# Row-tiled projections placed between score and value units of an attention + gated-MLP kernel, with a rearranged first head and a four-slot tail

## The chip, the cores and the metric

The kernel runs on one core of one Trainium2 chip. The metric is the device time of one execution in microseconds (us), from the first instruction to the last; a kernel's time is the median of its runs. The engines are PE (TensorE matmuls), PEld (weight loads, which overlap PE), DVE (VectorE), ACT (ScalarE), POOL (GpSimd) and SP (SyncE, which starts DMAs).

## The reference

```python
xn  = layernorm(x)                                   # x: 1 x 2048 x 640, bf16
q   = xn @ wq                                        # 32 heads of 192
p   = softmax(q @ k^T * 192**-0.5)                   # k, v caches: 32 heads x 2048 x 192
s   = concat_heads(p @ v) @ wo
h   = silu(xn @ w1) * (xn @ w3)                      # 640 -> 1536
out = x + s * silu(h @ w2)
```

## The kernel before

The kernel walks over a stream of units `(h, qb, p)`: head, block of 512 queries, pair of 128-key tiles. A block is eight pairs, and there are 32 x 4 = 128 blocks. Per pair, PE computes scores into one slot of a PSUM ring (two slots of two banks, pool `ps_st`), ACT takes the exponential, and two pairs later PE multiplies by the values into `obank`, a PSUM tile of four banks. Scores and values use only 64 rows of the array per matmul, so both run in *row tiles*: matmuls on rows 0 to 63 and on rows 64 to 127 go side by side.

```python
    ps_st = main.enter_context(tc.tile_pool(name="ps_st", bufs=2, space=bass.MemoryType.PSUM))
    ps_o  = main.enter_context(tc.tile_pool(name="ps_o", bufs=1, space=bass.MemoryType.PSUM))

    def project(h, qb, half):                       # full array: 5 matmuls over 128 rows
        ...
        ps = ps_st.tile([P, 1024], F32, tag="st2", name="ps")
        for c in range(DC):
            w = L["wqB"][:, c, :] if half else L["wq"][:, c, 0:P]
            nc.tensor.matmul(ps[:, 0:512], lhsT=w, rhs=xnT[:, c, qs], start=(c == 0), stop=(c == DC - 1))
        if half:
            nc.scalar.copy(out=qAB[:, 1, qs], in_=ps[:, 0:512])
        else:
            nc.vector.tensor_copy(out=qAB[:, 0, qs], in_=ps[:, 0:512])
        ...

    def values(n):
        h, qb, p = stream[n]
        if p == 0:
            obanks[0] = ps_o.tile([P, 2048], F32, tag="ob", name="obank")
        obank = obanks[0]
        ...                                         # 16 matmuls, r = 0 into banks 0-1, r = 1 into banks 2-3
        if p < NPAIR - 1:
            return
        ov = obank[:].rearrange("p (r j w) -> p r j w", r=2, j=4)
        osum = osp.tile([P, 4, DH + 1], F32, tag="osum", name="osum")
        nc.scalar.copy(out=osum[:], in_=ov[:, 0, :, 0:DH + 1])
        nc.vector.tensor_tensor(out=osum[:], in0=ov[:, 1, :, 0:DH + 1], in1=osum[:], op=ALU.add)

    for n, (h, qb, p) in enumerate(stream):
        scores(n + 2)
        values(n)
        ...                                         # head 0: LayerNorm and projection of its next block
        if p < NPAIR - 1:
            continue
        if h + 1 < H:
            project(h + 1, qb, 1)                   # both halves at the end of the block
            project(h + 1, qb, 0)
        finish_values(h, qb)
        if h < 2 * NPIG:
            swiglu(h, qb)                           # even heads: tanh on ACT, product on DVE
        loads_after(h, qb)
```

`obank` has one buffer. The first value unit of a block may therefore start only when both halves of the last block's `obank` have been read.

## Time and profile before

| | before |
|---|---|
| time, median (range of 4 runs) | 2004.1 us (2002.2 to 2005.1) |
| PE busy, granted clock | 98%, 0.994 |
| period of a block, heads 1 to 30 | 12.884 us |
| head 0 (from the start to the score unit of head 1's third pair, the first after all work of head 0) | 100.62 us |
| tail (from the first `ps_gu` matmul at 1692.78 us to the end) | 307.8 us |

The period is the distance of two equal PE rows of neighbouring blocks. From the page of the kernel before, the busy times and the chain of work that ended last:

```profile
PE 1966.2 (98%) x26025; PEld 1306.8 (65%) x26025; DVE 529.0 (26%) x862; ACT 1280.0 (64%) x1403; POOL 329.5 (16%) x561
...
PE 97%; DVE 2%; ACT 1%; issue 0%; DMA 0%; POOL 0%; DVEq 0%; ACTq 0%
```

The next fence is the timeline of PE before, at the end of a block (start in us, length in us, engine, line, operation, output and inputs, shapes, count):

```profile
1024.61 0.38 PE L343 MATMUL st_17867<-qAB,KA 64*128 64x512 bf16 x1
...
1025.26 0.83 PE L373 MATMUL obank<-vt_112,pT_17824 64*128 64x193 bf16 x16
1026.02 1.25 PE L297 MATMUL ps<-xnT,wqB 128*128 128x512 bf16 x5
1027.11 1.24 PE L297 MATMUL ps<-xnT,wq 128*128 128x512 bf16 x5
1028.28 0.39 PE L343 MATMUL st_17925<-qAB,KA 64*128 64x512 bf16 x1
...
1028.94 0.83 PE L373 MATMUL obank<-vt_113,pT_17849 64*128 64x193 bf16 x16
```

Read starts, not lengths, because matmuls are pipelined. A score unit takes 0.65 us, a value unit 0.67 us; from the last value unit of one block (1025.26) to the first of the next (1028.94) are 3.68 us. In that time `obank` must be read. Here is the timeline of ACT and DVE for it, in the same kernel:

```profile
1026.44 0.80 ACT L382 COPY osum<-obank 128x772 f32<-128x772 f32 x1
1027.27 0.96 DVE L383 TENSOR_TENSOR osum<-obank,osum 128x772 f32<-128x772 f32 x1 [9.28 <-ACT osum L382]
```

The bracket gives the idle time before a row and what ended it. The two reads follow each other; the second ends at 1028.23, before PE wants the bank at 1028.94. So in heads 1 to 30 the eviction is free. In head 31, which projects nothing, it isn't. From the list of waits of the kernel before (engine and output, who ended the wait, us in total, times, longest):

```profile
DVE qC L304 <- ACT qAB L299: 11.0, 4, 3.1
ACT ft L526 <- DVE hT L527: 9.9, 16, 0.6
ACT qC L306 <- DVE qAB L301: 6.0, 4, 1.5
PE obank L373 <- DVE osum L383: 4.6, 3, 1.6
```

In head 0, `qC` and `qAB` are both copies of one tile `ps`, and they read the same bank of it. In the tail, a tile `ps_f` has two parts; ACT takes the tanh `ft` of a part and DVE multiplies it into `hT`. The tanh of the second part needs nothing of the first part's product, and yet it waits for it in each of the 16 tiles, 0.62 us.

### The profile page before, as it was taken

The page shows a single profiled execution, that of the slowest core. Times are in us where ns is not written, and L with a number is a line of the kernel's source. Part 1 is how long each engine was busy: PE and PEld are TensorE (multiplying, and loading weights), DVE is VectorE, ACT ScalarE, POOL GpSimd, SP SyncE. Part 2 cuts the span into 40 slices and gives each one's busy share as a digit, 9 for nine tenths or more (in the row PEclk, how much of TensorE's full clock was granted, in tenths as well). Part 3 has the DMA queues.
Part 4 walks back from the last instruction along what each step waited for, and adds up shares of the span by engine and source line. Part 5 has one row for each costly group of instructions (what it writes and reads, how often), then busy time and mean ns, then how long its engine had stood idle before and what let it go on. Part 6 is the DMA issues. An engine that isn't in the chain of part 4 may idle for free.

```text
span 2000.6 us, 57142 instructions
## 1 busy us (share of the span) xinstructions
PE 1966.2 (98%) x26025; PEld 1306.8 (65%) x26025; DVE 529.0 (26%) x862; ACT 1280.0 (64%) x1403; POOL 329.5 (16%) x561
## 2 busy tenths in 40 slices
PE   7999999999999999999999999999999998999998
PEld 4566666666666666666666666666666666567776
DVE  5322222222222222222222222222222222521111
ACT  4677777777777777777777777777777776210000
POOL 2111111111111111111111111111111110000000
PEclk8999999999999999999999999999999999999999
DMA  7123332334333434363434343433233310908873
GB/s 153 34 61 92 65 99 64 95 65 98 68 99 68 99 68 99 67 162 68 100 68 99 68 99 68 97 66 99 68 91 77 64 53 25 253 20 148 152 147 60
DMA packets 361368, 177.43 MB, mean 89 GB/s; under 512 B 307360, under 2 KB 348064, under 8 KB 361120
## 3 DMA queue, kind: packets, MB, share of 16 engines
q1 hardware_dynamic: 335984, 114.96, 26.7%
q0 software_dynamic: 22832, 56.13, 11.7%
q8 instruction: 205, 3.36, 0.8%
q10 hardware_dynamic: 2304, 2.62, 0.5%
q14 instruction: 43, 0.35, 0.1%
HBM read 54.66 MB, written 27.79 MB: 41 GB/s over the span
## 4 chain that ended last, share of the span: by engine, by line
PE 97%; DVE 2%; ACT 1%; issue 0%; DMA 0%; POOL 0%; DVEq 0%; ACTq 0%
PE obank L373 34%; PE ps L297 14%; PE ps_s L102 10%; PE ps_f L521 3%; PE ps_gu L492 1%; PE ps_gu L495 1%; DVE stats L262 0%; PE pst L279 0%; DMA x_all<-in_A_x_dram 0%; DVE qAB L301 0%; DVE osum L383 0%; ACT osum L382 0%; DVE mv L263 0%; ACT qC L306 0%; DVE qC L307 0%
## 5 line engine op out<-in xcount | busy, mean ns | idle before, releaser
L383 DVE TENSOR_TENSOR osum<-obank,osum 128x772 f32<-128x772 f32 x128 | 123.2, 962 | 1178.6 <-ACT osum L382 1178.6
L309 POOL DMA_DIRECT2D qC<-qAB x248 | 132.2, 533 | 1288.4 <-ACT qAB L299 1207.8
L102 PE MATMUL ps_s<-wo_sb,oT 128*128 128x256 bf16 (+1 forms) x1536 | 208.8, 299 | 2.2 <-issue 2.2
L102 PEld LDWEIGHTS <-oT 128*128 128x128 bf16 x1536 | 150.2, 98 | 60.5 <-issue 2.2
L343 PEld LDWEIGHTS <-KC 64*128 64x128 bf16 x1024 | 96.5, 94 | 123.5 <-ACT KC L231 2.0
L297 PE MATMUL ps<-xnT,wqB 128*128 128x512 bf16 x640 | 161.4, 383 | 1.0 <-DVE xnT L282 1.0
L297 PE MATMUL ps<-xnT,wq 128*128 128x512 bf16 x640 | 159.4, 380 | 0.0
L343 PEld LDWEIGHTS <-KA 64*128 64x128 bf16 x1024 | 96.2, 94 | 56.2 <-issue 55.8
L390 DVE TENSOR_TENSOR ostage<-osum,rl_all 128x768 bf16<-128x768 f32 x128 | 122.6, 958 | 4.4
L297 PEld LDWEIGHTS <-wq 128*128 128x128 bf16 x640 | 62.8, 98 | 76.1 <-issue 1.0
L382 ACT COPY osum<-obank 128x772 f32<-128x772 f32 x128 | 102.0, 797 | 0.9 <-PE obank L373 0.9
L344 PEld LDWEIGHTS <-KA 64*128 64x128 bf16 x1024 | 96.1, 94 | 3.6 <-issue 3.5
L344 PEld LDWEIGHTS <-KB 64*128 64x128 bf16 x1024 | 96.6, 94 | 0.4 <-issue 0.4
L343 PEld LDWEIGHTS <-KB 64*128 64x128 bf16 x1024 | 96.6, 94 | 0.3 <-issue 0.3
L344 PEld LDWEIGHTS <-KC 64*128 64x128 bf16 x1024 | 96.5, 94 | 0.0
L297 PEld LDWEIGHTS <-wqB 128*128 128x128 bf16 x640 | 52.3, 98 | 67.2 <-issue 22.2
L301 DVE CAST qAB<-ps 128x512 bf16<-128x512 f32 x128 | 88.6, 692 | 19.3 <-PE ps L297 19.2
L299 ACT CAST qAB<-ps 128x512 bf16<-128x512 f32 x128 | 75.0, 586 | 14.0 <-PE ps L297 5.4
L311 POOL DMA_DIRECT2D qC<-qAB x124 | 65.0, 524 | 0.3 <-issue 0.3
L107 DVE SCALAR_TENSOR_TENSOR tmp<-ps_s,hT 128x384 f32<-128x384 f32 (+1 forms) x32 | 15.6, 488 | 179.6 <-PE ps_s L102 179.6
L521 PE MATMUL ps_f<-w_all,hT 128*128 128x384 bf16 (+1 forms) x384 | 52.3, 299 | 0.0
L98 POOL DMA_DIRECT2D xt<-in_A_x_dram x16 | 8.6, 540 | 256.1 <-DVE res L110 256.1
(9272 smaller groups left out, 5448.1 us busy)
## 6 DMA issues: line engine op xcount, KB each, us to landing
o_scr<-ostage SPq DMA_DIRECT2D x16, 1536.0 KB, 9.3
qC<-qAB POOLq DMA_DIRECT2D x372, 64.0 KB, 1.9
vt_112<-in_A_v_cache_dram SPq DMA_DIRECT2D x16, 768.0 KB, 6.6
vt_113<-in_A_v_cache_dram SPq DMA_DIRECT2D x16, 768.0 KB, 6.4
wq<-in_A_wq_dram POOLq DMA_DIRECT2D x32, 240.0 KB, 3.6
wo_sb<-in_A_wo_dram POOLq DMA_DIRECT2D x1, 7680.0 KB, 39.2
KC<-KA POOLq DMA_DIRECT2D x31, 128.0 KB, 5.8
KC<-KB POOLq DMA_DIRECT2D x31, 128.0 KB, 6.0
```

The source lines that it names most:

```text
L102: nc.tensor.matmul(ps[:, b * 512:b * 512 + c1 - c0], lhsT=oT[:, k, :], rhs=wo_sb[:, k, c0:c1], start=(k == 0), stop=(k == OC - 1))
L297: nc.tensor.matmul(ps[:, 0:512], lhsT=w, rhs=xnT[:, c, qs], start=(c == 0), stop=(c == DC - 1))
L299: nc.scalar.copy(out=qAB[:, 1, qs], in_=ps[:, 0:512])
L301: nc.vector.tensor_copy(out=qAB[:, 0, qs], in_=ps[:, 0:512])
L309: nc.gpsimd.dma_start(out=qC[0:64, half, qs], in_=qAB[64:P, half, qs])
L343: nc.tensor.matmul(st2[:, 0:512], lhsT=k0, rhs=q0, start=r == 0, stop=r == 2)
L344: nc.tensor.matmul(st2[:, 512:1024], lhsT=k1, rhs=q1, start=r == 0, stop=r == 2)
L373: nc.tensor.matmul(obank[:, o0:o0 + DH + 1], lhsT=pT2[r * 64:(r + 1) * 64, t * 512 + j * P:t * 512 + (j + 1) * P], rhs=vt[r * 64:(r + 1) * ...
L382: nc.scalar.copy(out=osum[:], in_=ov[:, 0, :, 0:DH + 1])
L383: nc.vector.tensor_tensor(out=osum[:], in0=ov[:, 1, :, 0:DH + 1], in1=osum[:], op=ALU.add)
L390: nc.vector.tensor_tensor(out=ostage[:, qb * 4:qb * 4 + 4, hg * DH:(hg + 1) * DH], in0=osum[:, :, 0:DH], in1=rl.unsqueeze(2).to_broadcast( ...
L521: nc.tensor.matmul(ps[:, b * 512:b * 512 + c1 - c0], lhsT=hT[:, fc, i * P:(i + 1) * P], rhs=w2_sb[:, fc, c0:c1], start=(fc == 0), stop=(fc ...
```

## The change

The intent: take the changes between row tiles and the full array out of every block by projecting in row tiles, and hide the accumulator's eviction under one half of a projection; give head 0 its LayerNorm statistics a block ahead and a warmed-up PE; use four PSUM slots in the tail.

```diff
 def project(h, qb, half):
         ps = ps_st.tile([P, 1024], F32, tag="st2", name="ps")
+        if h == 0: ...                              # as before
+        else:
+            for c in range(DC):
+                for r in range(2):
+                    rows = slice(r * 64, (r + 1) * 64)
+                    nc.tensor.matmul(ps[:, r * 512:(r + 1) * 512], lhsT=w[rows, c, 0:P], rhs=xnT[rows, c, qs],
+                                     start=(c == 0), stop=(c == DC - 1))
+            part = hbp.tile([P, 512], F32, tag="part", name="part")
+            nc.scalar.copy(out=part[:], in_=ps[:, 0:512])
+            nc.vector.tensor_tensor(out=dst, in0=ps[:, 512:1024], in1=part[:], op=ALU.add)
 ...
         nc.scalar.copy(out=osum[:], in_=ov[:, 0, :, 0:DH + 1])
-        nc.vector.tensor_tensor(out=osum[:], in0=ov[:, 1, :, 0:DH + 1], in1=osum[:], op=ALU.add)
+        nc.vector.tensor_copy(out=opart[:], in_=ov[:, 1, :, 0:DH + 1])
+        nc.vector.tensor_tensor(out=osum[:], in0=osum[:], in1=opart[:], op=ALU.add)
 ...
     for n, (h, qb, p) in enumerate(stream):
         scores(n + 2)
+        if h + 1 < H and p == (5 if h == 0 else 0):
+            project(h + 1, qb, 1)
+        if h + 1 < H and p == (NPAIR - 1 if h == 0 else NPAIR // 2):
+            project(h + 1, qb, 0)
         values(n)
+        if p == 0 and n > 0:
+            finish_block(n - 1)
+        if p == 2 and h < 2 * NPIG:
+            swiglu(h, qb)
         if h == 0 and qb + 1 < NQB:
-            ...
+            if p == 1 or p == 2:
+                ln_norm(qb + 1, p - 1)
+            if p == 3:
+                project(0, qb + 1, 1); project(0, qb + 1, 0)
+            if qb + 2 < NQB and 3 <= p < 7:
+                ln_stats(qb + 2, p - 3)
 # cut: longer PE warm-up, KC copies ahead of the first projection, head 0's qC by DMA from block 1 on;
 # tail: ps_gu, ps_f and ps_s alternate between ps_st and a second pool on obank's banks,
 #       the count matmul moves from after ps_f to its fifth tile, the last output tile is cut 512 + 128
```

More of the change, by code (lines that the diff above doesn't have):

```diff
@@ L90, in _exact_attention, with _output_stage @@
                 nc.sync.dma_start(out=o_scr[qs, bass.ds(h * DH, DH)], in_=ob[:])
-def _output_stage(nc, i, oT, g, wo_sb, x2, out2, sb, ps_pool):
+def _output_stage(nc, i, oT, g, wo_sb, x2, out2, sb, ps_pools, last=False):
     D = out2.shape[1]
     OC = wo_sb.shape[1]
+    cuts = [(0, D - P), (D - P, D)] if last and D - P <= 512 else _column_pieces(D)
     xt = sb.tile([P, D], BF16, tag="xt", name="xt")
     nc.gpsimd.dma_start(out=xt[:], in_=x2[i * P:(i + 1) * P, :])
-    ps = ps_pool.tile([P, 1024], F32, tag="st2", name="ps_s")
-    for b, (c0, c1) in enumerate(_column_pieces(D)):
-        for k in range(OC):
-            nc.tensor.matmul(ps[:, b * 512:b * 512 + c1 - c0], lhsT=oT[:, k, :], rhs=wo_sb[:, k, c0:c1],
-                             start=(k == 0), stop=(k == OC - 1))
     tmp = sb.tile([P, D], F32, tag="tmp", name="tmp")
     res = sb.tile([P, D], BF16, tag="res", name="res")
-    for b, (c0, c1) in enumerate(_column_pieces(D)):
+    for b, (c0, c1) in enumerate(cuts):
+        w = c1 - c0
+        ps = ps_pools[b % len(ps_pools)].tile([P, 1024], F32, tag="st2", name="ps_s")
+        for k in range(OC):
+            nc.tensor.matmul(ps[:, 0:w], lhsT=oT[:, k, :], rhs=wo_sb[:, k, c0:c1], start=(k == 0), stop=(k == OC - 1))
         nc.vector.scalar_tensor_tensor(out=tmp[:, c0:c1].rearrange("p (a w) -> p a w", w=P),
-                                       in0=ps[:, b * 512:b * 512 + c1 - c0].rearrange("p (a w) -> p a w", w=P),
+                                       in0=ps[:, 0:w].rearrange("p (a w) -> p a w", w=P),
                                        scalar=0.5, in1=g[:, c0 // P:c1 // P, :], op0=ALU.mult, op1=ALU.mult)
         nc.vector.tensor_tensor(out=res[:, c0:c1], in0=tmp[:, c0:c1], in1=xt[:, c0:c1], op=ALU.add)
-    nc.scalar.dma_start(out=out2[i * P:(i + 1) * P, :], in_=res[:])
+        if last:
+            nc.scalar.dma_start(out=out2[i * P:(i + 1) * P, c0:c1], in_=res[:, c0:c1])
+    if not last:
+        nc.scalar.dma_start(out=out2[i * P:(i + 1) * P, :], in_=res[:])
 def _column_pieces(n):
@@ L188, in _kernel_impl @@
     hbp = att.enter_context(tc.tile_pool(name="hbp", bufs=2))
-    osp = att.enter_context(tc.tile_pool(name="osp", bufs=2))
+    osp = att.enter_context(tc.tile_pool(name="osp", bufs=1))
     lnp = att.enter_context(tc.tile_pool(name="lnp", bufs=2))
     ps_st = main.enter_context(tc.tile_pool(name="ps_st", bufs=2, space=bass.MemoryType.PSUM))
-    ps_o = main.enter_context(tc.tile_pool(name="ps_o", bufs=1, space=bass.MemoryType.PSUM))
+    ps_o = att.enter_context(tc.tile_pool(name="ps_o", bufs=1, space=bass.MemoryType.PSUM))
     x_all = fw.tile([P, WX], BF16, tag="xw", name="x_all")
@@ L230, in copy_k @@
             nc.scalar.copy(out=KC[64:P, :], in_=KA[0:64, HK:SK])
-            nc.scalar.copy(out=KC[0:64, :], in_=KB[64:P, 0:HK])
+            nc.vector.tensor_copy(out=KC[0:64, :], in_=KB[64:P, 0:HK])
         else:
@@ L252, in _kernel_impl, with ln_stats @@
     lnorm = {}
-    def ln_stats(g):
-        mv = lnp.tile([P, 4, nc.vector.BN_AGGR_DIM], F32, tag="mv", name="mv")
-        ve = lnp.tile([P, 4], F32, tag="ve", name="ve")
-        rstd = lnp.tile([P, 4], F32, tag="rstd", name="rstd")
-        for i in range(4):
-            stats = lnp.tile([P, nsub, nc.vector.BN_STATS_DIM], F32, tag="stats", name="stats")
-            xr = x_sb[:, 4 * g + i, :].rearrange("p (a f) -> p a f", a=nsub)
-            for a in range(nsub):
-                nc.vector.bn_stats(out=stats[:, a, :], in_=xr[:, a, :])
-            nc.vector.bn_aggr(out=mv[:, i, :], in_=stats[:])
-            if i % 2 == 1:
-                two = slice(i - 1, i + 1)
-                nc.vector.tensor_scalar(out=ve[:, two], in0=mv[:, two, 1], scalar1=eps, scalar2=None, op0=ALU.add)
-                nc.gpsimd.tensor_tensor(out=rstd[:, two], in0=ve[:, two], in1=mhalf[:, two], op=ALU.pow)
-        lnorm[g] = (mv, rstd)
+    def ln_stats(g, i):
+        if i == 0:
+            lnorm[g] = [lnp.tile([P, 4, n], F32, tag=t, name=t)
+                        for t, n in (("mv", nc.vector.BN_AGGR_DIM), ("ve", 1), ("rstd", 1))]
+        mv, ve, rstd = lnorm[g]
+        stats = lnp.tile([P, nsub, nc.vector.BN_STATS_DIM], F32, tag="stats", name="stats")
+        xr = x_sb[:, 4 * g + i, :].rearrange("p (a f) -> p a f", a=nsub)
+        for a in range(nsub):
+            nc.vector.bn_stats(out=stats[:, a, :], in_=xr[:, a, :])
+        nc.vector.bn_aggr(out=mv[:, i, :], in_=stats[:])
+        if i % 2 == 1:
+            two = slice(i - 1, i + 1)
+            nc.vector.tensor_scalar(out=ve[:, two, 0], in0=mv[:, two, 1], scalar1=eps, scalar2=None, op0=ALU.add)
+            nc.gpsimd.tensor_tensor(out=rstd[:, two, 0], in0=ve[:, two, 0], in1=mhalf[:, two], op=ALU.pow)
     def ln_norm(g, i2):
-        mv, rstd = lnorm[g]
+        mv, _, rstd = lnorm[g]
         pst = ps_st.tile([P, 2, DC, P], BF16, tag="st2", name="pst")
@@ L275, in ln_norm @@
             xn = lnp.tile([P, D], BF16, tag="xn", name="xn")
-            nc.vector.tensor_scalar(out=xn[:], in0=x_sb[:, 4 * g + i, :], scalar1=mv[:, i, 0:1], scalar2=rstd[:, i:i + 1],
+            nc.vector.tensor_scalar(out=xn[:], in0=x_sb[:, 4 * g + i, :], scalar1=mv[:, i, 0:1], scalar2=rstd[:, i, 0:1],
                                     op0=ALU.subtract, op1=ALU.mult)
@@ L293, in project @@
         qs = slice(qb * 512, (qb + 1) * 512)
+        dst = qAB[:, half, qs]
+        w = L["wqB"] if half else L["wq"]
         ps = ps_st.tile([P, 1024], F32, tag="st2", name="ps")
-        for c in range(DC):
-            w = L["wqB"][:, c, :] if half else L["wq"][:, c, 0:P]
-            nc.tensor.matmul(ps[:, 0:512], lhsT=w, rhs=xnT[:, c, qs], start=(c == 0), stop=(c == DC - 1))
-        if half:
-            nc.scalar.copy(out=qAB[:, 1, qs], in_=ps[:, 0:512])
-        else:
-            nc.vector.tensor_copy(out=qAB[:, 0, qs], in_=ps[:, 0:512])
-        if h == 0 and half:
-            nc.vector.tensor_copy(out=qC[0:64, 1, qs], in_=ps[64:P, 0:512])
-        elif h == 0:
-            nc.scalar.copy(out=qC[0:64, 0, qs], in_=ps[64:P, 0:512])
-            nc.vector.tensor_copy(out=qC[64:P, 0, qs], in_=ps[0:64, 0:512])
+        if h == 0:
+            for c in range(DC):
+                nc.tensor.matmul(ps[:, 0:512], lhsT=w[:, c, 0:P], rhs=xnT[:, c, qs], start=(c == 0), stop=(c == DC - 1))
+            copy = nc.scalar.copy if half else nc.vector.tensor_copy
+            copy(out=dst, in_=ps[:, 0:512])
+        else:
+            for c in range(DC):
+                for r in range(2):
[5 more added lines that the diff above has]
+            nc.vector.tensor_tensor(out=dst, in0=ps[:, 512:1024], in1=part[:], op=ALU.add)
+        if h == 0 and qb == 0:
+            if half:
+                nc.vector.tensor_copy(out=qC[0:64, 1, qs], in_=ps[64:P, 0:512])
+            else:
+                nc.scalar.copy(out=qC[0:64, 0, qs], in_=ps[64:P, 0:512])
+                nc.vector.tensor_copy(out=qC[64:P, 0, qs], in_=ps[0:64, 0:512])
         else:
@@ L381, in values @@
         osum = osp.tile([P, 4, DH + 1], F32, tag="osum", name="osum")
+        opart = osp.tile([P, 4, DH + 1], F32, tag="opart", name="opart")
         nc.scalar.copy(out=osum[:], in_=ov[:, 0, :, 0:DH + 1])
-        nc.vector.tensor_tensor(out=osum[:], in0=ov[:, 1, :, 0:DH + 1], in1=osum[:], op=ALU.add)
+        nc.vector.tensor_copy(out=opart[:], in_=ov[:, 1, :, 0:DH + 1])
+        nc.vector.tensor_tensor(out=osum[:], in0=osum[:], in1=opart[:], op=ALU.add)
         osums[0] = osum
@@ L393, in loads_after @@
     def loads_after(h, qb):
-        if qb == max(1, NQB - 2) and h + 2 < H:
+        if qb == NQB - 2 and h + 2 < H:
             load_w(h + 2)
@@ L417, in loads_after, with turn_over @@
                 )
-    warm = ps_st.tile([P, 1024], F32, tag="st2", name="warm")
-    for i in range(56):
-        nc.tensor.matmul(warm[:, 0:P], lhsT=ident_bf[:], rhs=ident_bf[:], start=True, stop=True)
+    warm = ps_o.tile([P, 2048], F32, tag="ob", name="warm")
+    def turn_over(k):
+        for i in range(k):
+            nc.tensor.matmul(warm[:, 0:P], lhsT=ident_bf[:], rhs=ident_bf[:], start=True, stop=True)
     load_x(0)
@@ L426, in _kernel_impl @@
     load_k(0)
-    ln_stats(0)
+    for i in range(4):
+        ln_stats(0, i)
     load_v(0)
@@ L430, in _kernel_impl @@
         load_x(g)
+    turn_over(88)
     ln_norm(0, 0)
     ln_norm(0, 1)
+    turn_over(12)
+    copy_k(0)
     project(0, 0, 1)
     project(0, 0, 0)
-    copy_k(0)
-    ln_stats(1)
+    turn_over(8)
+    for i in range(4):
+        ln_stats(1, i)
     scores(0)
@@ L441, in _kernel_impl, with finish_block @@
     scores(1)
+    def finish_block(n):
+        h, qb, _ = stream[n]
+        finish_values(h, qb)
+        loads_after(h, qb)
     for n, (h, qb, p) in enumerate(stream):
         scores(n + 2)
+        if h + 1 < H and p == (5 if h == 0 else 0):
+            project(h + 1, qb, 1)
+        if h + 1 < H and p == (NPAIR - 1 if h == 0 else NPAIR // 2):
+            project(h + 1, qb, 0)
         values(n)
-        if h == 0 and qb + 1 < NQB:
-            if p == 0 and qb > 0:
-                ln_stats(qb + 1)
-            if p == NPAIR - 6:
-                ln_norm(qb + 1, 0)
-            if p == NPAIR - 5:
-                ln_norm(qb + 1, 1)
-            if p == NPAIR - 4:
+        if p == 0 and n > 0:
+            finish_block(n - 1)
+        if p == 2 and h < 2 * NPIG:
+            swiglu(h, qb)
+        if h == 0 and qb == 0 and p == NPAIR - 1:
+            copy_k(1)
+        if h == 0 and qb + 1 < NQB:
+            if p == 1 or p == 2:
+                ln_norm(qb + 1, p - 1)
+            if p == 3:
                 project(0, qb + 1, 1)
                 project(0, qb + 1, 0)
-        if p < NPAIR - 1:
-            continue
-        if h + 1 < H:
-            if h == 0 and qb == 0:
-                copy_k(1)
-            project(h + 1, qb, 1)
-            project(h + 1, qb, 0)
-        finish_values(h, qb)
-        if h < 2 * NPIG:
-            swiglu(h, qb)
-        loads_after(h, qb)
+            if qb + 2 < NQB and 3 <= p < 7:
+                ln_stats(qb + 2, p - 3)
+    finish_block(len(stream) - 1)
     att.close()
@@ L473, in _kernel_impl @@
     fsb = main.enter_context(tc.tile_pool(name="fsb", bufs=2))
+    ps_t = main.enter_context(tc.tile_pool(name="ps_t", bufs=2, space=bass.MemoryType.PSUM))
+    pools = (ps_st, ps_t)
     wo_sb = wop.tile([P, OC, D], BF16, name="wo_sb")
@@ L489, in _kernel_impl @@
         for fl in range(FC - FCP):
-            ps = ps_st.tile([P, 1024], F32, tag="st2", name="ps_gu")
+            ps = pools[(qb * (FC - FCP) + fl) % 2].tile([P, 1024], F32, tag="st2", name="ps_gu")
             for c in range(DC):
@@ L517, in _kernel_impl @@
     for i in range(NQT):
-        ps = ps_st.tile([P, 1024], F32, tag="st2", name="ps_f")
+        ps = pools[i % 2].tile([P, 1024], F32, tag="st2", name="ps_f")
         for fc in range(FC):
@@ L529, in _kernel_impl @@
                                            in1=pv.rearrange("p (a w) -> p a w", w=P), op0=ALU.add, op1=ALU.mult)
-    cnt = ps_st.tile([P, 1024], F32, tag="st2", name="cnt")
-    nc.tensor.matmul(cnt[0:2, 0:2], lhsT=ones[:], rhs=okb[:], start=True, stop=True)
-    tot = fsb.tile([1, 1], F32, tag="tot", name="tot")
-    nc.vector.tensor_reduce(out=tot[:], in_=cnt[0:1, 0:2], axis=AX.X, op=ALU.add)
-    nc.vector.tensor_copy(out=flag[:], in_=tot[:])
+        if i == 4:
+            cnt = ps_st.tile([P, 1024], F32, tag="st2", name="cnt")
+            nc.tensor.matmul(cnt[0:2, 0:2], lhsT=ones[:], rhs=okb[:], start=True, stop=True)
+            tot = fsb.tile([1, 1], F32, tag="tot", name="tot")
+            nc.vector.tensor_reduce(out=tot[:], in_=cnt[0:1, 0:2], axis=AX.X, op=ALU.add)
+            nc.vector.tensor_copy(out=flag[:], in_=tot[:])
     for i in range(NQT):
@@ L537, in _kernel_impl @@
             load_oT(i + 2, otp)
-        _output_stage(nc, i, oTs[i], g_of(i), wo_sb, x2, out2, fsb, ps_st)
+        _output_stage(nc, i, oTs[i], g_of(i), wo_sb, x2, out2, fsb, pools, last=i == NQT - 1)
     main.close()
@@ L550, in _kernel_impl @@
                 load_oT(i, ot2)
-                _output_stage(nc, i, oTs[i], g_of(i), wo_sb, x2, out2, sb2, ps2)
+                _output_stage(nc, i, oTs[i], g_of(i), wo_sb, x2, out2, sb2, (ps2,))
 @with_exitstack
```

## The prediction

> **What bounds it now.** The page gives TensorE (PE) 98% busy at a granted clock near 1, and the chain of waits is 97% PE. Only PE time counts. By the timeline, a block (one head, 512 queries) repeats every 12.884 us: eight score-and-value pairs of 1.3145 us (10.516) and two 128-row projections. The projections start 0.10 us late after the last value unit and take 2.26 us to the next score unit; ten matmuls at 0.2155 us are 2.155. So changing between row tiles and the full array costs 0.21 us a block, 26 us in 124 blocks. The Trainium skill, "TensorEngine Tiling (Array Packing)", Key Properties, has a mode change drain the engine; the gaps agree.
>
> Outside that: head 0's first block runs at half clock until about 26 us; its blocks 1 and 2 take 22.86 us each (PE idle 4.1 us). In head 31, without projections, the waits show 1.55 us per block for DVE's osum add. In the tail: 1.52 us for the PSUM ring in ps_gu, 2.16 us before the first ps_s, four DVE operations (about 2 us) after the last matmul.
>
> **What the change does, costed.**
> 1. Heads 1 to 30 project in row tiles: twenty matmuls, two at a time, like the score units: a half is 5 x 0.2155 = 1.08 us. At most 26 us saved.
> 2. Price: per half an ACT copy (0.59 us), then a DVE add (0.70 us), in the score units' PSUM ring. An exp takes 1.02 us and ends about 1.93 us after its scores start; a projection wants its slot at 1.96. Chaining the trace's durations and hand-overs (0.05 us ACT to PE) gives waits of 0.06 us at the first half, 0.03 at the second half, 0.09 at a score unit after it (the osum copy delays an exp). In blocks of even heads the tanh (0.63 us on ACT, now at pair 2) delays the exp ahead of the second half: 0.17 instead of 0.03. Estimate: 12.74 us per block (odd heads), 12.87 (even). Saved in 120 blocks: 60 x 0.15 + 60 x 0.01 = about 10 us, not 26.
> 3. obank: ACT and DVE copy in parallel. In head 31 the wait falls from 1.5 to about 0.65 us: -2 us.
> 4. Head 0: warm clock and no wait for KC, but the second block's LayerNorm now waits for its statistics (x lands about 19 us, statistics until 24 us, PE wait 3 to 4 us): -4 us. Blocks 1 and 2 to about 17.7 us: -5 each. Block 3 loses about 0.6 (obank no longer hidden). Together -14 us.
> 5. Tail: -1.5 (four slots), -2.2 (count early), -1.2 (last piece 128 wide): -5 us.
>
> Sum: -10 - 14 - 2 - 5 = -31 us; I lean to smaller waits in 2. Predicted 1971 us, range 1957 to 1983. Chances: faster by over 2% 0.2, within 2% 0.79, slower by over 2% 0.01.
>
> **What would show it.** Block period in the timeline: 12.66 means no waits, 12.88 means everything given back. The waits should show PE ps <- ACT exp, longest at second halves of even heads. The score of head 1 should begin near 86 us instead of 100.6. Osum waits in head 31 near 0.65 us.
>
> **What would make it wrong.** Row-tiled halves slower than 1.08 us; hand-overs 0.05 us shorter or longer, worth 6 us or more; head 0 falling back to the half clock during its statistics wait; head 0's qC copies, now by DMA, landing late.

## The result

| | before | after |
|---|---|---|
| time, median (4 runs each) | 2004.1 us | 2059.6 us (2059.3 to 2060.9) |
| ratio, 95% interval | | 1.0279 (1.0262 to 1.0297) |
| granted clock | 0.994 | 0.998 |
| block period, odd / even heads | 12.884 us | 13.35 / 13.46 us |
| head 0 (to the same point) | 100.62 us | 100.75 us |
| heads 1 to 31 | 1592.2 us | 1656.6 us |
| tail | 307.8 us | 300.7 us |

Ratios here are the mean time of one kernel's fast runs over that of the other's in the same rounds, so not quite the ratio of the quoted medians. The changed kernel is 2.8% slower; forecast was 1.6% faster. The stages come from the traces (spans 2000.6 and 2058.1 us): head 0 +0.1, heads 1 to 31 +64.5, tail -7.1, together +57.5.

The page of the changed kernel, the lines shown of before:

```profile
PE 1974.5 (96%) x27317; PEld 1380.7 (67%) x27317; DVE 727.6 (35%) x1109; ACT 1316.3 (64%) x1523; POOL 333.0 (16%) x570
...
PE 80%; DVE 7%; issue 6%; ACT 6%; SPq 1%; DMA 0%; ACTq 0%; DVEq 0%
```

DVE and ACT are in the chain of work that ended last now, with 13% between them. The timeline of PE after, around the first pair of a block:

```profile
1025.22 0.85 PE L386 MATMUL obank<-vt,pT 64*128 64x193 bf16 x16
1025.89 0.38 PE L356 MATMUL st<-qAB,KA 64*128 64x512 bf16 x1
...
1026.57 1.26 PE L309 MATMUL ps<-xnT,wqB 64*128 64x512 bf16 x10
1028.26 0.84 PE L386 MATMUL obank<-vt,pT 64*128 64x193 bf16 x16 [0.43 <-DVE opart L397]
1028.92 0.38 PE L356 MATMUL st<-qAB,KA 64*128 64x512 bf16 x1
```

The row-tiled half costs what was forecast: where nothing waits, the next unit starts 1.08 us after it (1020.20 to 1021.28 in the same trace). But the value unit starts 1.69 us after this half began, 0.61 us later than 1.08. (The 0.43 in the bracket counts from the modelled end of the last matmul, so it is smaller than the loss between starts.) ACT and DVE in the same stretch:

```profile
1026.42 0.80 ACT L396 COPY osum<-obank 128x772 f32<-128x772 f32 x1
1027.24 0.96 DVE L397 COPY opart<-obank 128x772 f32<-128x772 f32 x1 [4.44 <-ACT osum L396]
```

The two copies, which share no data, run one after the other. The second ends at 1028.20, and PE starts at 1028.26. The list of waits of the changed kernel:

```profile
DVE opart L397 <- ACT osum L396: 565.7, 128, 8.4
PE obank L386 <- DVE opart L397: 61.5, 126, 1.5
```

All 128 copies of `opart` wait for ACT, and 126 of 128 blocks make PE wait for them. The eviction still takes the same 1.8 us as before, but PE wants the bank after a score unit and one half of a projection instead of after two halves and a score unit.

### The profile page after: what moved, and what is told of

Its sections match the earlier page's. It is cut to its first block, busy times and chain, and to the rows that moved or that the text cites. A ratio compares the mean times of both kernels' runs of the same rounds, so it can differ in the third digit from the quotient of the medians.

```text
span 2058.1 us, 60051 instructions
## 1 busy us (share of the span) xinstructions
PE 1974.5 (96%) x27317; PEld 1380.7 (67%) x27317; DVE 727.6 (35%) x1109; ACT 1316.3 (64%) x1523; POOL 333.0 (16%) x570
## 4 chain that ended last, share of the span: by engine, by line
PE 80%; DVE 7%; issue 6%; ACT 6%; SPq 1%; DMA 0%; ACTq 0%; DVEq 0%
PE obank L386 30%; PE st L356 25%; PE ps_s L106 10%; PE ps L309 7%; DVE opart L397 6%; ACT osum L396 5%; PE st L357 3%; PE ps_f L549 3%; PE ps_gu L520 1%; PE ps_gu L523 1%; ACT pT L359 1%; DMA x_all<-in_A_x_dram 0%; PE ps L302 0%; SPq L226 0%; PE pst L281 0%
## 5 line engine op out<-in xcount | busy, mean ns | idle before, releaser
L359 ACT ACTIVATE pT<-st 128x1024 bf16<-128x1024 f32 x1024 | 1048.7, 1024 | 431.8 <-PE st L357 431.8
L386 PEld LDWEIGHTS <-pT 64*128 64x128 bf16 x16384 | 742.5, 94 | 296.2 <-issue 100.3
L386 PE MATMUL obank<-vt,pT 64*128 64x193 bf16 x16384 | 867.0, 244 | 61.5 <-DVE opart L397 61.5
L356 PE MATMUL st<-qAB,KA 64*128 64x512 bf16 x1024 | 385.7, 377 | 1.8 <-DVE qAB L304 1.8
L357 PE MATMUL st<-qC,KC 64*128 64x512 bf16 x1024 | 386.2, 377 | 0.1
L357 PE MATMUL st<-qAB,KA 64*128 64x512 bf16 x1024 | 386.3, 377 | 0.0
L357 PE MATMUL st<-qAB,KB 64*128 64x512 bf16 x1024 | 386.3, 377 | 0.0
L356 PE MATMUL st<-qC,KB 64*128 64x512 bf16 x1024 | 385.8, 377 | 0.1
L356 PE MATMUL st<-qC,KC 64*128 64x512 bf16 x1024 | 385.8, 377 | 0.0
L313 DVE TENSOR_TENSOR qAB<-ps,part 128x512 bf16<-128x512 f32 x248 | 170.6, 688 | 381.0 <-ACT part L312 381.0
L106 PE MATMUL ps_s<-wo_sb,oT 128*128 128x256 bf16 (+3 forms) x1536 | 208.8, 300 | 0.0
L309 PE MATMUL ps<-xnT,wq 64*128 64x512 bf16 x1240 | 155.8, 377 | 0.6 <-ACT pT L359 0.6
```

The lines of the kernel that those rows point to most:

```text
L106: nc.tensor.matmul(ps[:, 0:w], lhsT=oT[:, k, :], rhs=wo_sb[:, k, c0:c1], start=(k == 0), stop=(k == OC - 1))
L309: nc.tensor.matmul(ps[:, r * 512:(r + 1) * 512], lhsT=w[rows, c, 0:P], rhs=xnT[rows, c, qs], start=(c == 0), stop=(c == DC - 1))
L313: nc.vector.tensor_tensor(out=dst, in0=ps[:, 512:1024], in1=part[:], op=ALU.add)
L356: nc.tensor.matmul(st2[:, 0:512], lhsT=k0, rhs=q0, start=r == 0, stop=r == 2)
L357: nc.tensor.matmul(st2[:, 512:1024], lhsT=k1, rhs=q1, start=r == 0, stop=r == 2)
L359: nc.scalar.activation(out=pT2[:], in_=st2[:], func=ACT.Exp, scale=att_scale)
```

## The experiments

Theory A: the two reads of `obank` are serialised because they read one PSUM tile, and that deadline costs about 0.6 us per block (the expectations below have it as 0.55). Rival B: row-tiled projections themselves are dear, through their two evictions in the score ring.

### e1: the accumulator as two tiles

```diff
-            obanks[0] = ps_o.tile([P, 2048], F32, tag="ob", name="obank")
+            for r in range(2):
+                obanks[r] = ps_o.tile([P, 1024], F32, tag=f"ob{r}", name=f"obank{r}")
 ...
-                    o0 = r * 1024 + j * 256
-                    nc.tensor.matmul(obank[:, o0:o0 + DH + 1], ...
+                    o0 = j * 256
+                    nc.tensor.matmul(obanks[r][:, o0:o0 + DH + 1], ...
-        ov = obank[:].rearrange("p (r j w) -> p r j w", r=2, j=4)
+        ov = [obanks[r][:].rearrange("p (j w) -> p j w", j=4) for r in range(2)]
# cut: the two copies read ov[0] and ov[1]; the warm-up tile takes the first of the two tiles
```

> The changed kernel with the value accumulator as two PSUM tiles of two banks, one read by ACT and one by DVE, so that neither read waits for the other; nothing else changes. Theory A (the two evictions of one tile are made to run one after the other, 0.80 + 0.96 us, and one projection half of 1.08 us plus a score unit does not cover that): the wait of the first value unit falls from about 0.55 us to nearly 0 in heads 1 to 30, from 1.5 to about 0.65 us in head 31, the block period goes from 13.35 (odd heads) and 13.46 (even) to 12.74 and 12.87, and the time to about 1981 us (1974 to 1988). Rival B (the row-tiled projection itself is dear: two evictions, contention in the score ring): the wait only moves elsewhere and the time stays over 2040 us.

Measured: 1982.5 us, ratio to before 0.9892 (0.9876 to 0.9909). In the built program the wait of the `opart` copy, which had been on ACT, is now on PE. The timeline of DVE and ACT in e1:

```profile
1022.86 0.96 DVE L397 COPY opart<-obank 128x772 f32<-128x772 f32 x1 [3.32 <-PE obank L386]
1023.16 0.80 ACT L396 COPY osum<-obank 128x772 f32<-128x772 f32 x1
```

and of PE:

```profile
1023.32 1.26 PE L309 MATMUL ps<-xnT,wqB 64*128 64x512 bf16 x10
1024.39 0.85 PE L386 MATMUL obank<-vt,pT 64*128 64x193 bf16 x16
```

The copies overlap, each at its old length, and the value unit follows its projection half after 1.07 us. The same four banks, the same instructions and the same bytes give 77 us back. Periods are 12.74 (odd) and 12.85 us (even), as A expected. Heads 1 to 31 take 1580.0 us in this trace, 12.2 less than before, where the prediction had -12. B falls.

### e2: row tiles at the old place

Edit: the kernel before, with the `project` of the change (and one buffer for `osum`); both halves stay after the last value unit.

> The kernel before with one part of the change: projections of heads 1 to 31 in row tiles with the ACT copy and the DVE add, both halves at the old place after the last value unit. Theory A: PE work per block falls by 0.21 us, but the slot of the first half is wanted again after one projection half, and its DVE add stands behind the accumulator's eviction; chaining the trace's durations gives a wait of 0.8 us per block at the next score unit, a period of 13.50 us and about 2079 us (2065 to 2090). A rival that blames only the new places would have this version faster than before, near 1978 us.

Measured: 2077.2 us, ratio 1.0368 (1.0351 to 1.0385), period 13.48 us. The timeline shows why (PE and DVE rows):

```profile
1030.26 1.26 PE L305 MATMUL ps<-xnT,wqB 64*128 64x512 bf16 x10
...
1031.34 1.26 PE L305 MATMUL ps<-xnT,wq 64*128 64x512 bf16 x10
...
1031.62 0.96 DVE L391 TENSOR_TENSOR osum<-obank,osum 128x772 f32<-128x772 f32 x1 [9.48 <-ACT osum L390]
1032.50 1.45 DVE L309 TENSOR_TENSOR qAB<-ps,part 128x512 bf16<-128x512 f32 x2
...
1033.24 0.37 PE L351 MATMUL st<-qAB,KA 64*128 64x512 bf16 x1 [0.64 <-DVE qAB L309]
```

The next score unit needs the slot of the first half, whose DVE add stands behind the accumulator's. So row tiling alone is no gain either: its second eviction needs a place with time behind it, which is what the new places give.

### e3: the tail alone

Edit: the kernel before with the changed `_output_stage` and everything after the attention.

> The kernel before with only the changed tail (four PSUM slots, early count, last tile cut 512 + 128). From the two traces, tail spans of 307.8 and 300.2 us: 7.6 us faster than before, about 1996.5 us (1995 to 1998).

Measured: 1995.2 us, ratio 0.9958 (0.9941 to 0.9975); its tail takes 300.75 us (1691.75 to 1992.5). That is 7.1 us less than before, as in the changed kernel, and a little more than the 5 us forecast. The rest of the 8.3 us between the medians isn't the tail's: in e3's trace head 0, which has no edit, is 1.0 us shorter too.

### e4 and e9: full-array projections at the new places

Edit: in the changed kernel (e4) and in e1 (e9), `if h == 0:` in `project` becomes `if True:`, so every half is five full-array matmuls and one eviction.

> The changed kernel with full-array projections (five matmuls and one eviction per half, as before) at the new places. Theory A: four changes of tiling mode per block instead of none, 0.42 us of PE time, but the deadline of the accumulator's eviction stays, so its wait falls from 0.55 to about 0.40; period about 13.55 us, time about 2076 us (2062 to 2088), slower than the changed kernel. Rival B (row tiling's second eviction is what costs): faster than the changed kernel, under 2050 us.

> e4 with the accumulator in two tiles (equally: e1 with full-array projections at the new places). With the accumulator's wait gone nothing hides the changes of tiling mode: four per block, 0.42 us, against none in e1, and one eviction per half less. Theory: period about 13.17 us against 12.74 to 12.84 in e1, time about 2026 us (2018 to 2034), so that row tiles are worth about 44 us at these places. If row tiling gives nothing by itself: within 5 us of e1.

Measured: e4 2077.1 us, ratio 1.0370 (1.0352 to 1.0387), period 13.55 us in the even head looked at; e9 2019.3 us, ratio 1.0080 (1.0064 to 1.0095), period 13.10 to 13.12 us. e4's wait is still there, as one row of its PE timeline shows:

```profile
1038.15 0.84 PE L386 MATMUL obank<-vt,pT 64*128 64x193 bf16 x16 [0.37 <-DVE opart L397]
```

Without row tiles, e4 is 17 us slower than the changed kernel, and e9 is 37 us slower than e1 (2019.3 against 1982.5, from two sets of rounds). So row tiling pays at these places, by 0.3 us a block where nothing hides it; the accumulator's wait swallowed half of that in the changed kernel, because a deadline set by DVE doesn't move when PE gets there sooner.

### e10: the two tiles in the kernel before

Edit: the kernel before with e1's tiles and the change's `opart` copy (and one buffer for `osum`).

> The kernel before with only the accumulator in two tiles and the parallel eviction (opart). There the eviction stands behind two projection halves and a score unit (2.9 us), so in heads 0 to 30 it should gain nothing, and in head 31 three waits fall from 1.55 to about 0.65 us: 2 to 3 us faster, about 2001 us. If serial eviction costs something in every block of the kernel before too, it is over 20 us faster.

Measured: 1999.9 us, ratio 0.9983 (0.9969 to 0.9997). Serial copies cost the kernel before almost nothing: two projection halves hid them, and the period is still 12.88 us. Only in head 31, which has no projections, did the period fall, from 12.24 to 11.24 us. It was the new place that laid them bare.

### e5: tanh at another pair

```diff
-        if p == 2 and h < 2 * NPIG:
+        if p == (2 if h == 0 else 5) and h < 2 * NPIG:
```

(on e1)

> e1 with one line changed: from head 1 the swiglu step (a 0.63 us tanh on ACT in even heads) stands at pair 5 instead of pair 2, so it no longer delays the exp whose PSUM slot the second projection half takes. Theory: blocks of even heads fall from 12.84 to 12.74 us, the period of odd heads; 60 blocks, 6 to 8 us, about 1976 us. If the tanh has nothing to do with that wait: no change, 1982.5.

Measured: 1974.7 us, ratio 0.9851 (0.9836 to 0.9866), against 0.9892 for e1. Blocks of even heads now have 12.74 us, as those of odd heads do. The forecast of a wait at the second half in even heads was right: it was 0.11 us a block instead of 0.14.

### e6: head 0's LayerNorm ahead of swiglu

```diff
-        if p == 2 and h < 2 * NPIG:
+        if h > 0 and p == 2 and h < 2 * NPIG:
             swiglu(h, qb)
         if h == 0 and qb + 1 < NQB:
             ...                                    # ln_norm(qb + 1, p - 1) at p == 1, 2
+        if h == 0 and p == 2:
+            swiglu(h, qb)
```

(on e1)

> e1 with the swiglu step of head 0 issued after the second LayerNorm half of the next block instead of before it. Theory: PE waits 2.40 us in each of three blocks because DVE, in order, holds the second pair of xn behind the swiglu product, which waits for a tanh that stands behind an exp on ACT; with the order turned the waits go to under 0.5 us, head 1 starts about 6 us earlier and the time is about 1976 us. Rival: the statistics or the arrival of x are what is late; then the waits stay at about 2.4 us.

The reason for this run lies in the timeline of the changed kernel, head 0, ACT, DVE and PE:

```profile
26.87 1.23 ACT L284 COPY xnT<-pst 128x1280 bf16<-128x1280 bf16 x1 [2.26 <-PE pst L281]
27.99 1.03 ACT L359 ACTIVATE pT<-st 128x1024 bf16<-128x1024 f32 x1
28.90 0.62 ACT L335 ACTIVATE pt<-qAB 64x512 bf16<-64x512 bf16 x1
29.55 0.68 DVE L336 SCALAR_TENSOR_TENSOR hT<-pt,qAB 64x512 bf16<-64x512 bf16 x1 [3.23 <-ACT pt L335]
30.16 0.79 DVE L278 TENSOR_SCALAR xn<-x_all,mv,rstd 128x640 bf16<-128x640 bf16 x2
...
30.65 0.81 PE L281 MATMUL pst<-ident_bf,xn 128*128 128x128 bf16 x10 [2.40 <-DVE xn L278]
```

DVE takes these two in the order in which they were issued. The product `hT` waits for a tanh that stands behind a copy and an exponential on ACT, and `xn`, whose buffers came free with the first transposes at 26.8 us, waits behind it until 30.16. This happens in each of the three blocks with a LayerNorm. After the second of them the trace shows matmuls at half their rate (from 50 to 60 us the granted clock averages 0.83):

```profile
53.28 1.50 PE L386 MATMUL obank<-vt,pT 64*128 64x193 bf16 x16
54.71 2.18 PE L302 MATMUL ps<-xnT,wqB 128*128 128x512 bf16 x5
56.73 1.24 PE L302 MATMUL ps<-xnT,wq 128*128 128x512 bf16 x5
```

Measured in e6: 1973.8 us, ratio 0.9850 (0.9835 to 0.9865). The second transposes no longer wait:

```profile
24.92 0.81 PE L281 MATMUL pst<-ident_bf,xn 128*128 128x128 bf16 x10 [2.32 <-DVE xn L278]
27.08 0.73 PE L281 MATMUL pst<-ident_bf,xn 128*128 128x128 bf16 x10
```

Head 1's first projection half starts at 91.94 us instead of 101.39 in e1. Of those 9.5 us, 1.6 were there at the first transposes already (24.92 against 26.48 us), ahead of the edit's effect; the other 7.9 are the three waits of 2.40 and the half-rate stretch (about 1.5 us, by the distances of the transposes in the two traces), less about 0.8 that e6 lost in the first of the three blocks, 0.57 of it in a wait for the DMA of `wqB`. The stretch is gone too (granted clock 1.00 from 50 to 60 us). That the waits bring it about is likely, not shown: in the changed kernel the third wait, as long as the second, is followed by full rate.

### e7 and e8: the parts together

e7 is e1 with the edits of e5 and e6, and in head 0's blocks 1 to 3 the halves for head 1 at pairs 0 and 5. e8 moves the load of the second quarter of x ahead of the first values.

> e1 with both of those, and in head 0's blocks 1 to 3 the halves for head 1 at pairs 0 and 5 instead of 5 and 7, to hide the accumulator's eviction there too. Sum of the parts: -6 (tanh), -6 (order), -1 to -2 (places): about 1968 us (1965 to 1971), faster than both kernels, 1.8% under the kernel before.

> e7 with the second quarter of x loaded ahead of the first values instead of behind them, because the statistics of the second block began only when it landed, at 21 us. If that arrival is on the chain: 1 to 2 us less than e7, about 1966.5 us. If the values then come late for the first value unit instead: equal or up to 1 us more.

Measured: e7 1964.7 us, ratio 0.9804 (0.9791 to 0.9818); e8 1965.0 us, ratio 0.9806 (0.9793 to 0.9820). e7 is faster than both kernels, by 39 us than the one before; that it is 2% faster can't be said, since the interval has 0.98 in it. In its trace head 0's blocks 1 and 2 take 17.9 and 18.1 us, near the 17.7 of the prediction. e8 shows no difference. The moment at which the first keys and x land differs from trace to trace: the copy of `KB` started at 15.63 us in the changed kernel, 16.61 in e1 and 13.87 in e7, whose loads are the same. Why, no run tells; a gain of a microsecond at that point can't be told from it.

All ten kernels gave correct results.

## Why the prediction was wrong

- **What bounds the kernel: right.** PE's time, with 0.21 us per block for changing between row tiles and the full array. The Trainium skill, "TensorEngine Tiling (Array Packing)", Key Properties, says that a change of tiling mode drains the engine. The traces show a loss at each change: in e9 each half stands about 0.1 us from its neighbours on both sides, and e9 against e1 puts four such changes a block, less other waits, at 0.3 us. That draining is what takes this time, no run shows apart from that.
- **Step 1 (1.08 us per half): right.** 1.08 us measured.
- **Step 2 (waits for the score ring): right in kind; its period owes something to luck.** With the accumulator's wait removed, e1 has 12.74 and 12.85 us where 12.74 and 12.87 were forecast, and e5 removed the tanh term. In e1's blocks a half starts 0.05 us after an exponential ends, whatever the head, so this wait exists: 0.04 us before each half, 0.15 before the second half in even heads (forecast 0.06, 0.03 and 0.17). The wait of 0.09 at a score unit didn't appear. As listed, the waits of the odd heads add up to 0.18 us, while 12.74 leaves only 0.08 above the 12.66 without waits: the list and the period of the prediction don't agree, so that the period came out right owes something to luck.
- **Step 3 failed, and it decides the result.** It read: "obank: ACT and DVE copy in parallel." They do not. Both read one tile, and the built program makes the second reader wait for the first: 128 of 128 `opart` copies waited for ACT. The forecast chain therefore had `obank` free at the right time in heads 1 to 30, a wait of zero that the text didn't even list, and 0.65 us in head 31. Measured: 0.61 us lost in a block of heads 1 to 30, and still up to 1.5 us in head 31. The prediction gave a result over 2% slower a chance of 0.01. e1, which alters only the tiles, moves the time by 77 us; the miss in heads 1 to 31 was 76 us (-12 forecast, +64.5 measured). This is shown, not argued.
- It could have been seen beforehand. In the trace of before, ACT and DVE wait for each other where they read one PSUM tile. The `qC` rows above can't tell whether the tile or the bank is the reason, since both copies read one bank. The `ft` row can: there the two engines read different banks of `ps_f`, and ACT still waited for DVE, 16 times of 16. The forecast took it that two copies without a common result run together.
- The Trainium skill, "PSUM — Partial Sum Buffer", Specifications, says that ScalarE and VectorE can read PSUM in parallel as long as they do not meet in a bank. e1 agrees: 0.96 and 0.80 us, overlapping, at unchanged lengths. The banks were distinct in the changed kernel too, so hardware wasn't what kept the copies apart there; it was the wait.
- **Step 4 (head 0, -14 us) failed:** +0.1 measured. The wait for the statistics was foreseen; not foreseen was that `swiglu` at pair 2 stands ahead of the second LayerNorm half in DVE's order. Three waits of 2.40 us came of it, and e6 took about 8 us back. The forecast's -5 us for each of the blocks 1 and 2 took away the waits that PE had there before, 4.10 us a block (3.22 for `xn`, 0.32 and 0.56 for `qC`), but others of 4.05 took their place (2.40 and 0.41 for `xn`, 1.24 for `obank`):

```profile
49.37 0.99 PE L279 MATMUL pst<-ident_bf,xn 128*128 128x128 bf16 x10 [3.22 <-DVE xn L276]
...
44.65 0.84 PE L386 MATMUL obank<-vt,pT 64*128 64x193 bf16 x16 [1.24 <-DVE opart L397]
47.21 0.81 PE L281 MATMUL pst<-ident_bf,xn 128*128 128x128 bf16 x10 [0.41 <-DVE xn L278]
51.85 0.81 PE L281 MATMUL pst<-ident_bf,xn 128*128 128x128 bf16 x10 [2.40 <-DVE xn L278]
```

The first row is of the kernel before, the others are of the changed one. Block 3 has the 1.24 us too, where 0.6 was forecast. Nor did the first scores come earlier (17.64 us against 17.51 before): the copy of `KB` waited 2.7 us for its DMA, and matmuls ran at half rate from 19.0 to 22.7 us, where the prediction had a warm clock.

- **Step 5 (tail, -5 us): right in kind, small by 2 us:** -7.1 in the traces of the changed kernel and of e3.

## What to carry to other kernels

Before counting on two engines to read one PSUM tile side by side, look in the trace for a pair that already does so; if one waits for the other though they read different banks, give each reader its own tile. When work that covers an eviction is moved, work out when the buffer comes free and what still stands before its next use: the eviction did not get slower here, its cover went from 3.7 to 2.4 us between value units. When an instruction is put into an in-order engine's stream, ask what it waits for, and what stands behind it.

## What the Trainium skill lacked or had wrong

- "PSUM — Partial Sum Buffer", Specifications, tells that two engines can read PSUM in parallel in different banks; no page tells that two readers of different banks of one tile may be made to wait for each other by the program as built. It cost 77 us of 2060 here (e1), and the cure is one tile per reader.
- "TensorEngine Tiling (Array Packing)", Key Properties, says that a mode change drains the engine and gives no size. Here it cost about 0.1 us each: 0.21 us for two changes in the kernel before.
- "TensorEngine Tiling (Array Packing)", PSUM Bottleneck, advises both ScalarE and VectorE for evacuating PSUM. It could say that this shortens nothing unless the two can run at once (0.80 + 0.96 us in series in the changed kernel, about 1.1 us from the first start to the last end in e1).
